# adaLN linear-attention block with a SiLU MLP on one core: first modulation columns as matrix products, later modulation sums by 32 by 32 transposes, and a new order table

## The chip, the core and the metric

The kernel runs on one core of one Trainium2 chip. The metric is the device time of one execution in microseconds (us). Every time below is from the runs of the kernel before the change, or from the profile of one of its executions.

## The reference

Inputs: `x` (2048 x 576), `wqkv` (576 x 1728), `wo` (576 x 576), `w1` (576 x 4608), `w2` (4608 x 576), `c` (1 x 576), `w_mod` (576 x 3456), all float32.

```python
mod = (silu(c) @ w_mod).reshape(1, 6, 1, 576)
sa, ca, ga, sb, cb, gb = (mod[:, i] for i in range(6))
h = layernorm(x) * (1 + ca) + sa
x = x + ga * linear_attention(h, wqkv, wo)     # 32 heads of 18, phi(t) = (t+1 if t>0 else exp(t)) + 1e-6
h = layernorm(x) * (1 + cb) + sb
x = x + gb * (silu(h @ w1) @ w2)
```

## The kernel before

**Tiling.** The 2048 rows are 16 tiles of 128, in four blocks of four. The width 576 is cut into five chunks k: four of 128 and a tail of 64, which is kept twice (128 wide) so that every chunk fills the partitions. Projections use pairs of values (a rounded part and the rest), so that each float32 product is made of several passes. In the trace one true float32 product (`x8` warm-ups in the program, say) appears as two matmul records, a transpose or a pass on rounded operands as one.

**Stages.** (1) The start: `c` goes through silu, the first two rows of the modulation (sa, ca; piece 0) are needed as columns (`cols["a"]`) because h is used transposed, tiles 0 and 1 are normalised, transposed on TensorE (`turn_tiles`), modulated (`modulate`, L355 to L361) and split (`split_h`), and their K projections run chunk by chunk (`first_k`, `k_lo`, `k_part` at L573). (2) The rest of the attention (to about 196 us): K projections of all tiles and Q projections of tiles 0 to 10 (L928), sums over tokens (L1053, added up on VectorE at L1063), the other pieces of the modulation (`mod_steps`, L1090: piece 1 is ga and sb, piece 2 is cb and gb), then `kv_steps` (L1178), whose mask is applied on VectorE at L1193, and `m_steps` (L1215), which multiplies the masked result with `wo`. (3) Attention outputs and second normalisation (to about 355 us). (4) The MLP, in 18 groups of 256 columns by two pairs of blocks (L1924, L2008), to the end.

**The start in detail.** `mods[k]` holds rows of `w_mod` for chunk k, `sc` is silu(c), `tmod` the tail rows, `sel` two columns that pick the two halves of the tail. `HEAD` = 2 chunks come first. The sum over k is made on VectorE: `add_rows` (L516, L518) multiplies `mods[k]` with its column of `sc` and adds into `sums`; then a product with a column of ones (`mod_cols`, L523 and L527) sums over partitions and yields columns of chunks 0 and 1. For chunks 2 to 4 the same sums give two rows on one partition (`mod_rows`, L538), these are copied to SBUF (`copy_row`), and turned into columns by six transposes of one row (`turn_rows`, L549). `add_cols` (L532) adds the 1 of (1 + ca). `keep_busy(n)` (L567) issues n products of ones, whose results nobody reads.

**Pieces 1 and 2.** `mod_steps` scales each chunk on ScalarE, adds chunks on GpSimd into `tmod` (128 partitions x 1152), stores it to DRAM (`parts`, L1104), loads it back so that each partition holds nine columns of all 128 partitions (L1107), reduces over them on VectorE (L1110), and stores `vec` (L1111).

**Order.** Inside stage 2 a table (`STAGE_A`) says in which order the steps of a small planner are issued. After the program is written, `arrange(ORDERS, begun)` takes, for each engine, the list of its instructions and ties them to the order of a second table of numbers, `ORDERS`, which reaches from the start into the first MLP units. Instructions on one engine wait in that order.

Of the kernel before, what the change touches and what calls it, by code (L numbers as in the profile page):

```python
# [24 lines left out]
def kernel(ctx: ExitStack, tc, A_x, A_wqkv, A_wo, B_x, B_w1, B_w2, c, w_mod, out):  # L25
# [33 lines left out]
    def behind(instructions):  # L59

        with ExitStack() as order:
# [7 lines left out]
            0-43 45-46 52 49-50 44 47-48 53-54 51 65 57-58 61-62 66-72 55-56 59-60 63-64 73-77 82-83 80-81 78-79  # L69
            84-87 90-91 88-89 92-101 116-118 102-103 124 104-105 119-123 125 106-115 126-141 154-167 142-153  # L70
            168-181 246-251 210-213 182-199 214-215 290-293 216-219 294-295 200-209 220-221 256-267 274-277
            222-223 278-289 224-237 302-307 238-245 252-255 308-311 268-273 330-335 296-301 336-357 312-319
            358-359 320-325 360-367 326-329 368-375 378-383 376-377 386-389 384-385 398-403 390-393 404-405
            394-397 412-423 436-451 406-411 424-435 452-477 490-499 478-489 524-527 500-513 520-523 530-539
            514-519 586-587 528-529 588-589 540-545 554-571 576-579 592-597 590-591 598-599 610-621 600-609
            546-551 646-647 580-581 622-627 582-585 552-553 572-575 648-657 670-671 628-641 672-675 682-683
            642-645 684-687 714-721 658-663 722-723 664-665 692-693 666-669 688-689 694-713 724-725 676-679
            726-727 690-691 728-729 680-681 742-745 730-741 746-791 826-831 792-795 862-863 796-797 864-867
            832-833 872-873 798-813 838-839 814-815 840-853 816-821 854-855 822-823 856-859 874-877 860-861
            868-871 878-889 834-837 890-895 824-825 896-917 926-935 918-921 936-939 922-923 940-947 924-925  # L80
            978-983 1000-1003 950-955 966-975 1004-1005 976-977 984-993 948-949 994-999 1006-1019 1022-1023
            1020-1021 956-965 1024-1035 1050-1055 1036-1049 1056-1063 1084-1085 1064-1077 1102-1105 1086-1087
            1106-1113 1078-1079 1114-1117 1088-1091 1118-1123 1130-1131 1080-1081 1132-1135 1124-1129 1136-1137
            1082-1083 1138-1155 1096-1099 1092-1095 1160-1169 1156-1157 1170-1171 1100-1101 1172-1183 1158-1159
            1184-1219 1236-1237 1248-1259 1220-1221 1285-1286 1222-1227 1238-1247 1228-1235 1287-1296 1260-1262
            1297-1300 1263-1284 1301-1325 1352-1356 1326-1349 1357-1364 1385-1388 1365-1370 1389-1390 1350-1351
            1371-1384 1413-1416 1391-1400 1417-1427 1401-1406 1428-1429 1407-1412 1430-1443 1446-1449 1444-1445
            1451-1468 1450 1479-1486 1469-1478 1507-1511 1487-1506 1512-1535 1540-1544 1536-1539 1545-1568
            1573-1574 1569-1572 1575-1592 1601-1604 1593-1594 1605-1621 1595-1596 1634 1638 1597-1600 1622-1633
            1646-1649 1635-1636 1650 1639-1641 1655-1660 1687-1696 1637 1661-1676 1642-1645 1677-1682 1715-1719  # L90
            1697-1700 1651-1654 1701-1704 1683 1705-1706 1720-1723 1684-1686 1707-1714 1724-1751 1762-1767
            1776-1779 1781-1782 1768-1769 1780 1752-1753 1783-1794 1754-1761 1795-1798 1770-1772 1799-1800
            1773-1775 1801-1810 1821-1825 1854 1870-1873 1855-1857 1826-1835 1811-1820 1836-1843 1874 1858
            1875-1877 1844-1853 1859-1860 1883 1915 1884-1886 1861-1863 1916-1918 1878-1881 1887-1888 1882
            1864-1869 1889-1914 1919-1921 1931-1935 1976 1922-1927 1936-1939 1928-1930 1990-1993 1940-1941 1994
            1977-1978 1995-1996 1942-1971 2004-2007 1972-1975 1979-1982 2008-2010 1983-1984 2011-2012 1985-1988
            2013-2018 1989 2019-2036 1997-2003 2037 2049-2061 2082-2083 2098-2101 2062-2069 2086-2088 2070-2077
            2038-2045 2084-2085 2046-2048 2078-2081 2089 2102-2103 2090-2093 2106-2110 2094 2111-2112 2104
            2113-2114 2095-2097 2115-2122 2105 2123-2140 2143 2141-2142 2147 2159-2166 2144-2145 2167-2172 2146
            2173-2178 2187 2179-2186 2188 2199-2202 2189-2190 2203 2191 2204-2210 2213-2214 2148-2149 2215-2216  # L100
            2192-2198 2211-2212 2150-2158 2217 2231-2234 2218-2223 2235-2238 2224-2230 2239-2241 2249 2259-2262
            2245 2255-2258 2246-2248 2242 2263-2264 2243-2244 2265-2269 2295 2250 2296-2299 2251-2253 2270
            2309-2313 2254 2283 2271 2284-2285 2277-2278 2286-2293 2300 2294 2301-2302 2314 2303 2279 2304-2308
            2272-2276 2280-2282 2315-2324 2329 2335-2338 2325 2339-2340 2330-2331 2326-2328 2341 2332-2334
# [498 lines left out]
    for k in (1, 2, 3):  # L603
        add_rows(k, 0, c1)
# [1806 lines left out]
```

## Time and profile before

| | us |
|---|---|
| median of 3 runs | 1084.69 |
| lowest, highest | 1081.81, 1085.14 |
| the profiled execution, its own time | 1086.77 |
| its span in the trace | 1085.1 |
| TensorE busy in the span | 1063.3 |
| VectorE busy | 893.0 |
| ScalarE busy | 707.3 |
| GpSimd busy | 737.6 |

The profile names engines PE (TensorE matmul), PEld (its weight loads), DVE (VectorE), ACT (ScalarE), POOL (GpSimd) and SP (the queue that issues most DMAs). A row of a timeline has the start, the time from the first to the last end, engine, line, operation, output<-inputs and count; in brackets stands how long the engine was idle before it and who ended that. The profiled execution is 1.6 us longer than its span, and 2.1 us longer than the median.

### The profile page before, as it was taken

The page shows a single profiled execution, that of the slowest core. Times are in us where ns is not written, and L with a number is a line of the kernel's source. Part 1 is how long each engine was busy: PE and PEld are TensorE (multiplying, and loading weights), DVE is VectorE, ACT ScalarE, POOL GpSimd, SP SyncE. Part 2 cuts the span into 40 slices and gives each one's busy share as a digit, 9 for nine tenths or more (in the row PEclk, how much of TensorE's full clock was granted, in tenths as well). Part 3 has the DMA queues.
Part 4 walks back from the last instruction along what each step waited for, and adds up shares of the span by engine and source line. Part 5 has one row for each costly group of instructions (what it writes and reads, how often), then busy time and mean ns, then how long its engine had stood idle before and what let it go on. Part 6 is the DMA issues. An engine that isn't in the chain of part 4 may idle for free.

```text
span 1085.1 us, 19052 instructions
## 1 busy us (share of the span) xinstructions
PE 1063.3 (98%) x7027; PEld 760.6 (70%) x7027; DVE 893.0 (82%) x1438; ACT 707.3 (65%) x1318; POOL 737.6 (68%) x804
## 2 busy tenths in 40 slices
PE   8999999999999899999999999999999999999998
PEld 6999999898885455666666666666666666666665
DVE  7966857788889899988987988987987887898767
ACT  4866553248667777777667667767766776676554
POOL 3467524654725589879888778877778678677563
PEclk9999999999999999999999999999999999999999
DMA  8497954224256877387577577567667657626422
GB/s 294 143 178 202 101 148 119 70 83 127 61 165 195 240 250 254 125 250 230 175 223 213 182 217 222 171 223 203 200 196 234 201 154 252 206 68 201 165 80 109
DMA packets 119341, 193.50 MB, mean 178 GB/s; under 512 B 42892, under 2 KB 77584, under 8 KB 119248
## 3 DMA queue, kind: packets, MB, share of 16 engines
q1 hardware_dynamic: 86276, 190.81, 56.6%
q10 hardware_dynamic: 32972, 1.48, 3.1%
q8 instruction: 55, 0.90, 0.4%
q14 instruction: 38, 0.31, 0.1%
HBM read 176.77 MB, written 15.48 MB: 177 GB/s over the span
## 4 chain that ended last, share of the span: by engine, by line
PE 80%; DVE 9%; DMA 4%; ACT 2%; POOL 2%; issue 1%; SPq 0%; DVEq 0%; POOLq 0%; ACTq 0%
PE up L1924 31%; PE down L2008 30%; PE big L389 5%; PE psK L928 4%; PE psG L1053 4%; PE big L1443 2%; DMA raw<-parts 1%; DMA hT<-hd 1%; PE small L1432 1%; DVE hT L261 1%; PE small L374 1%; DMA raw<-in_w_mod_dram 1%; DVE w L261 1%; PE big L1357 1%; PE psK L1223 1%
## 5 line engine op out<-in xcount | busy, mean ns | idle before, releaser
L1924 PE MATMUL up<-hT,w 128*128 128x512 f16 x1264 | 317.9, 379 | 2.2 <-DMA hT<-hd 2.2
L1924 PEld LDWEIGHTS <-w 128*128 128x128 f16 x1492 | 145.8, 98 | 136.1 <-DMA hT<-hd 2.9
L2017 DVE SCALAR_TENSOR_TENSOR acc<-acc,set,down 128x576 f32<-128x576 f32 x128 | 103.6, 810 | 33.8 <-PE down L2008 32.9
L1942 ACT ACTIVATE f<-f,set 128x512 f32<-128x512 f32 x102 | 73.3, 719 | 63.6 <-DVE f L1948 52.1
L1962 POOL TENSOR_TENSOR s<-f,f 128x256 f32<-128x256 f32 x66 | 54.6, 827 | 77.4 <-ACT f L1943 75.3
L2008 PE MATMUL down<-w,hc 128*128 128x288 f16 x600 | 90.6, 286 | 0.1
L2008 PE MATMUL down<-w,hb 128*128 128x288 f16 x600 | 89.3, 286 | 0.6 <-DVE U L2019 0.5
L2008 PE MATMUL down<-w,hT 128*128 128x288 f16 x480 | 82.8, 286 | 0.4 <-DVE acc L2021 0.4
L1946 DVE TENSOR_TENSOR f<-up,p 128x512 f32<-128x512 f32 x102 | 69.6, 682 | 13.8 <-PE up L1924 9.4
L1943 ACT ACTIVATE f<-f,set 128x512 f32<-128x512 f32 x102 | 73.6, 722 | 3.2
L2008 PEld LDWEIGHTS <-hb 128*128 128x128 f16 x600 | 58.7, 98 | 22.7 <-issue 1.4
L2008 PEld LDWEIGHTS <-hc 128*128 128x128 f16 x600 | 58.7, 98 | 22.0 <-issue 0.4
L1986 POOL TENSOR_TENSOR hc<-s,hc 128x512 f16<-128x512 f32 x50 | 63.9, 1278 | 6.0 <-ACT hc L1982 6.0
L1948 DVE TENSOR_TENSOR f<-up,f 128x512 f32<-128x512 f32 x68 | 46.8, 689 | 25.4 <-PE up L1924 24.3
L2008 PEld LDWEIGHTS <-hT 128*128 128x128 f16 x480 | 46.9, 98 | 26.6 <-issue 0.8
L1966 POOL TENSOR_TENSOR f<-f,s 128x256 f32<-128x256 f32 x66 | 53.4, 809 | 17.3 <-DVE hb L1986 10.2
L1959 POOL TENSOR_TENSOR s<-f 128x256 f32<-128x256 f32 x66 | 57.0, 864 | 9.5 <-ACT f L1939 4.5
L1964 POOL TENSOR_TENSOR s<-s,f 128x256 f32<-128x256 f32 x66 | 56.3, 853 | 3.5
L389 PE MATMUL big<-w,qT 128*128 128x288 f32 x352 | 58.6, 304 | 0.0
L2008 PE MATMUL down<-w,hd 128*128 128x288 f16 x396 | 55.5, 286 | 0.2 <-DVE acc L2017 0.2
L2008 PE MATMUL down<-w,ha 128*128 128x288 f16 x396 | 55.7, 286 | 0.0
L1053 PE MATMUL psG<-w,xs 128*128 128x288 f32 x336 | 52.2, 296 | 1.3 <-DVE sum L1063 1.3
(408 smaller groups left out, 2805.3 us busy)
## 6 DMA issues: line engine op xcount, KB each, us to landing
hT<-hd SPq DMA_DIRECT2D x101, 640.0 KB, 4.6
hT<-hd SPq DMA_DIRECT2D x65, 512.0 KB, 3.7
hT<-in_B_w_dram SPq DMA_DIRECT2D x14, 576.0 KB, 6.4
hT<-in_B_w_dram SPq DMA_DIRECT2D x28, 256.0 KB, 5.8
raw<-in_B_w_dram SPq DMA_DIRECT2D x11, 576.0 KB, 6.2
v<-in_B_w_dram SPq DMA_DIRECT2D x9, 576.0 KB, 4.9
acc<-in_A_x_dram SPq DMA_DIRECT2D x16, 288.0 KB, 4.3
raw<-in_B_w_dram SPq DMA_DIRECT2D x9, 512.0 KB, 5.2
```

Source lines behind the costliest of these rows:

```text
L389: T.matmul(ps, xpart(a), wpart(b), start=n == 0, stop=n == len(XW) - 1)
L1053: T.matmul(ps[:, h, :HALF], l, pk[t][:, u, h * HALF : (h + 1) * HALF], start=t == 0 and m == 0, stop=t == 3 and m == len(left) - 1)
L1924: T.matmul(ps, left, right, start=first and m == 0, stop=m == len(seq) - 1, skip_group_check=True)
L1942: A.activation(f, f, AF.Silu, scale=factor(self.g, "inv"))
L1943: A.activation(f, f, AF.Identity, scale=factor(self.g, "delta"))
L1946: V.tensor_add(f, self.bank[bank[1]], self.p1)
L1959: G.tensor_sub(self.s3, half(i, 0, 0), half(i, 0, 1))
L1962: G.tensor_add(self.s[:, 0:1], half(i, 0, 1), half(i, 1, 1))
L1964: G.tensor_sub(self.s[:, 1:2], self.s[:, 0:1], half(i, 0, 0))
L1986: eng.tensor_sub(t[:, :, 1, :], src, t[:, :, 0, :])
L2008: T.matmul(ps[:, p, :HALF], left[:, u, p * P : (p + 1) * P], right[:, v], start=n in (1, 5, 7, 6) and j == 0, stop=j == len(passes) - 1, s ...
L2017: V.scalar_tensor_tensor(dst, dst, factor(self.g, "ratio"), ps[:, :, :HALF], op0=ALU.mult, op1=ALU.add)
```

## The change

Piece 0 is no longer summed on VectorE. Each of the five chunks of the two rows becomes a group of products whose stationary operand is a 128 x 128 block of `mods[k]` and whose moving operand is the column of `sc`, repeated 64 times (chunks 0 and 1) or 42 times (chunks 2 to 4); all land in one PSUM bank, and `add_cols` takes one of the equal columns. `twice` copies the 64 tail columns on GpSimd so that the last chunk is 128 wide. Rows, copies and one-row transposes go. For pieces 1 and 2, `tmod` is transposed in blocks of 32 by 32 on VectorE, reduced over groups of 32, transposed again, and only a 128 x 64 tile goes through DRAM (`quarters`) to add the four quarters. One weight load is issued ahead of two loads of `x`. `ORDERS` is a new table for all engines; `STAGE_A` stays.

```diff
     load_w(0, range(HEAD, KC))
+    load_w(0, [KC])
     xts += [load_x(i) for i in range(2, 4)]
-    load_w(0, [KC])
...
+    WIDE = 64, 42
+    def twice(m):
+        G.tensor_copy(m[..., D:DX], m[..., KC * P : D])
+    def mod_tail(js):
+        for j in js:
+            for a in range(2):
+                o = col(j, a)
+                T.matmul(o, tmod[:, j * P : (j + 1) * P], sel[:, a : a + 1].to_broadcast([P, o.shape[1]]),
+                         start=j == js[0] and a == 0, stop=False, skip_group_check=True)
+    def mod_part(k, js):
+        for j in js:
+            for a in range(2):
+                o = col(j, a)
+                T.matmul(o, mods[k][:, a, j * P : (j + 1) * P], sc[:, k : k + 1].to_broadcast([P, o.shape[1]]),
+                         start=False, stop=k == KC - 1, skip_group_check=True)
...
     keep_busy(11)
-    for k in range(HEAD):
-        mod_cols(k, tmod, sel, first=k == 0)
+    mod_tail(range(HEAD))
+    for k in range(KC):
+        mod_part(k, range(HEAD))
     turn_tiles(pT, (0, 1), START)
-    for k in (1, 2, 3):
-        add_rows(k, 0, c1)
+    keep_busy(4)
+    add_cols(0, HEAD)
...
+    twice(tmod)
+    mod_tail(range(HEAD, KC + 1))
+    for k in range(KC):
+        twice(mods[k])
+        mod_part(k, range(HEAD, KC + 1))
+        keep_busy(1)
+        if k < HEAD:
+            first_k(k)
     keep_busy(2)
+    add_cols(HEAD, KC + 1)
...
-        do("SP", 0.45, lambda: nc.sync.dma_start(parts, tmod2[:, :, 0:D]), ["tmod0", "tmod1"], [f"parts{piece}"], 8.0)
-        do("DVE", 2.27, lambda: V.tensor_reduce(s9, r.rearrange("q p j -> q j p"), axis=AX.X, op=ALU.add), raws2[i], [f"s9{piece}"])
+        def turn():
+            for a in range(2):
+                V.transpose(r[:, a].rearrange("p (b i) -> p b i", i=32), tmod2[:, a, 0:D].rearrange("p (b i) -> p b i", i=32))
+        def fold():
+            V.tensor_reduce(some[:, 0:NB32], flat.rearrange("p (b i) -> p b i", i=32), axis=AX.X, op=ALU.add)
+            V.transpose(turned_sums, some)
+            nc.sync.dma_start(quarters.rearrange("h p c -> p h c"), turned_sums.rearrange("p (h c) -> p h c", h=2))
+            for h in range(2):
+                n = (32, NB32 - 32)[h]
+                nc.sync.dma_start(four[32 * h : 32 * h + n], quarters[h].rearrange("(q b) c -> b q c", q=4)[:n])
+            V.tensor_reduce(total, four.rearrange("b q c -> b c q"), axis=AX.X, op=ALU.add)
```

**How the order moves: the start on TensorE.** The rows stand on TensorE behind the eleven warm-ups and the transposes of tiles 0 and 1, before the change (`psG_116`, `psG_117` and `psK` are PSUM, `xt` holds normalised rows of x, `hT` is the room of `mods` in products with `ones` or `sc`, and of h in products with `w`):

```order
L567 MATMUL psG_117<-ones 128x128 x4
L527 MATMUL psG_116<-ones,hT 128x1 x2
L567 MATMUL psG_117<-ones 128x128
L527 MATMUL psG_116<-ones,hT 128x1 x2
L567 MATMUL psG_117<-ones 128x128 x2
L573 MATMUL psK<-w,hT 128x288 x3
L538 MATMUL psG_116<-tmod,sc 1x320
L573 MATMUL psK<-w,hT 128x288 x7
L538 MATMUL psG_117<-tmod,sc 1x320
L538 MATMUL psG_117<-hT,ones 1x320
L573 MATMUL psK<-w,hT 128x288 x4
```

The end of the same stretch now, from the last groups of narrow products on (20 products 64 wide, ten transposes but one, and 18 products 42 wide stand ahead of these rows):

```order
L531 MATMUL psG_117<-sc,hT 128x42 x6
L542 MATMUL psG_116<-ident,xt 128x128
L553 MATMUL psG_117<-ones 128x128
L531 MATMUL psG_117<-sc,hT 128x42 x6
L553 MATMUL psG_117<-ones 128x128 x4
L1239 MATMUL psG_117<-ident,xt 128x128 x2
L559 MATMUL psK<-w,hT 128x288 x7
L1239 MATMUL psG_116<-ident,xt 128x128 x8
L559 MATMUL psK<-w,hT 128x288 x29
```

Before, the first projections (L573) stood between the steps that make the columns of chunks 2 to 4; now all 50 narrow products (20 of 64 columns, 30 of 42) stand ahead of the first projection (L559), and no projection waits for a column inside that stretch.

**The end of stage 2 on TensorE.** The rows are the last products of `kv_steps` and the first of `m_steps`, before:

```order
L1186 MATMUL psG_116<-sum_107,acc_94 72x72
L1186 MATMUL psG_116<-sum_108,acc_94 72x72
L1186 MATMUL psG_116<-sum_109,acc_94 72x72
L1186 MATMUL psG_116<-sum_110,acc_94 72x72
L1186 MATMUL psG_116<-sum_111,xt 72x72
L1223 MATMUL psK<-raw_121,tmod 128x288 x5
L1223 MATMUL psK<-raw_122,tmod 128x288
```

And now:

```order
L1175 MATMUL psG_116<-sum_109,acc_94 72x72
L1175 MATMUL psG_116<-sum_110,acc_94 72x72
L1175 MATMUL psG_116<-sum_111,xt 72x72
L901 MATMUL psK<-wq,hT 128x288 x12
L901 MATMUL psK<-v,hT 128x288 x4
L1212 MATMUL psK<-raw_121,tmod 128x288 x5
L1212 MATMUL psK<-raw_122,tmod 128x288
```

Sixteen passes of a Q projection, which stood ahead of `kv_steps` or among its products, now stand between its last product and the first of `m_steps`.

More of the change, by code (lines that the diff above doesn't have):

```diff
@@ L74 @@
[L74 to L78, printed above, removed]
@@ L186 @@
+            207
         """,
@@ L500 @@
     wk_ = wkp
-    sums = mods[0]
     sel = z[:, 2:4]
@@ L615 @@
     w_lo(wk_, 0, acc[0], G)
[L616 to L633 removed]
+    for k in range(HEAD):
+        modulate(*args[k], V)
+        split_h(*args[k])
+    w_hi(wk_, 1, acc[1])
+    w_lo(wk_, 1, acc[1], V)
+    twice(tmod)
[6 more added lines that the diff above has]
+            first_k(k)
+    keep_busy(2)
+    add_cols(HEAD, KC + 1)
     k_lo(0)
@@ L835, in follow @@
                         self.ops[queue.pop(0)][2]()
+                assert len(made) > before
         def emit(self):
@@ L1090, in mod_steps @@
     def mod_steps(piece):
-        parts, vec = parts_of[piece - 1], vec_of[piece - 1]
+        quarters, vec = quarters_of[piece - 1], vec_of[piece - 1]
         for k in START:
```

311 lines of the change are left out of this document (134 added, 177 removed).

## The prediction

> **What bounds the kernel now.** I read the page first, for the engine that fills the span.
>
> ```profile
> span 1085.1 us, 19052 instructions
> ...
> PE 1063.3 (98%) x7027; PEld 760.6 (70%) x7027; DVE 893.0 (82%) x1438; ACT 707.3 (65%) x1318; POOL 737.6 (68%) x804
> ```
>
> TensorE (PE) is busy for 1063.3 of 1085.1 us, so a gain can only come from the 21.8 us in which it is idle, from PE work that goes, or from a higher granted clock. The second view, busy time by stage, says where the idle time is (the columns are the stretch and its length, then PE, PEld, DVE, ACT and POOL busy, granted clock, DMA share, GB/s).
>
> ```profile
> 0.00:8.85 8.85, 7.46 (x39) 7.08 (x40) 3.35 (x17) 3.77 (x7) 1.44 (x8) 1.00 0.76 217
> 8.85:33.77 24.92, 21.27 (x132) 16.30 (x131) 22.08 (x46) 14.01 (x27) 10.05 (x7) 0.93 0.84 284
> 33.77:60.00 26.23, 25.50 (x188) 24.88 (x187) 21.84 (x35) 20.96 (x33) 15.87 (x11) 1.00 0.55 169
> ...
> 195.90:210.00 14.10, 12.17 (x62) 10.00 (x62) 11.01 (x28) 4.49 (x7) 6.66 (x7) 1.00 0.24 66
> ...
> 250.00:400.00 150.00, 142.59 (x947) 104.24 (x947) 133.81 (x231) 105.87 (x190) 82.45 (x90) 1.00 0.56 174
> 400.00:1000.00 600.00, 599.51 (x3801) 371.55 (x3799) 516.03 (x793) 422.97 (x841) 479.85 (x564) 1.00 0.64 201
> 1000.00:1085.10 85.10, 80.43 (x548) 53.31 (x546) 59.81 (x87) 44.73 (x75) 45.30 (x45) 1.00 0.35 120
> ```
>
> From 400 to 1000 us PE has 0.5 us left and nothing that an order table does there can matter. The idle time is 3.65 us in the start (24.92 less 21.27), 0.7 up to 60, 1.9 around 200, and 7.4 from 250 to 400, where VectorE (DVE) is busy for 133.81 of 150 us and is the engine waited for. The waits of PE by releaser agree:
>
> ```profile
> PE up L1924 <- DMA hT<-hd: 2.2, 1, 2.2
> PE big L1443 <- DVE acc L1448: 1.9, 1, 1.9
> PE psG L1053 <- DVE sum L1063: 1.3, 2, 0.7
> PE psK L1223 <- issue: 1.2, 1, 1.2
> ```
>
> The start also loses clock. A finer table shows PE 0.70 of 2 us busy from 18 to 20, and the clock at half from there to 24:
>
> ```profile
> 18.00:20.00 2.00, 0.70 (x2) 0.09 (x2) 2.00 (x2) 0.48 (x3) 1.85 (x2) 1.00 1.02 319
> 20.00:22.00 2.00, 1.81 (x6) 0.65 (x6) 1.93 (x7) 1.18 (x3) 0.00 (x0) 0.71 1.06 335
> 22.00:24.00 2.00, 2.00 (x9) 1.78 (x8) 1.24 (x4) 0.00 (x0) 1.69 (x2) 0.50 1.04 328
> ```
>
> **The start, step by step.** The stretch to price runs from the end of the eleven warm-ups (8.85) to the first pass of a Q projection at L928 (33.77). The same two points exist after the change, with all work between them in one line on PE. Its rows today:
>
> ```profile
> 8.85 0.58 PE L523 MATMUL psG<-z,tmod 128*128 128x2 f32 x4
> ...
> 10.69 0.44 PE L556 MATMUL psK<-ident,xt 128*128 128x128 f32 x2 [0.66 <-ACT xt L351]
> 10.97 0.49 PE L556 MATMUL psG<-ident,xt 128*128 128x128 f32 x3
> 11.29 1.06 PE L567 MATMUL psG<-ones 128*128 128x128 f32 x8
> 12.19 0.50 PE L527 MATMUL psG<-ones,hT 128*128 128x1 f32 x4
> 12.55 0.47 PE L567 MATMUL psG<-ones 128*128 128x128 f32 x2
> ```
>
> ```profile
> 28.19 2.38 PE L573 MATMUL psK<-w,hT 128*128 128x288 f32 x16 [0.20 <-DVE hT L261]
> 30.41 0.43 PE L573 MATMUL psK<-v,hT 128*128 128x288 f32 x2
> ...
> 31.79 0.82 PE L1250 MATMUL psG<-ident,xt 128*128 128x128 f32 x6
> 32.37 0.77 PE L573 MATMUL psK<-w,hT 128*128 128x288 f32 x4
> ...
> 33.77 0.47 PE L928 MATMUL psK<-wq,hT 128*128 128x288 f32 x2
> ```
>
> Durations overlap, so I price by the distance of starts. A float32 product is two records. With one moving column it takes (12.55 - 12.19)/2 = 0.18 us, with 128 columns (12.19 - 11.29)/4 = 0.225 us. The new products have 64 and 42 columns and lie between these: 0.18 to 0.225, and I take 0.20. A transpose takes (11.29 - 10.69)/5 = 0.12 us, one of the later ten (32.37 - 31.79)/6 = 0.10. A pass of a projection takes (30.41 - 28.19)/16 = 0.139 us.
>
> [...]
>
> After the change: 50 narrow products at 0.20 are 10.0 us; 10 transposes at 0.12 are 1.2; the warm-ups between them (4, three single ones, 4: eleven) at 0.225 are 2.5; ten later transposes at 0.10 are 1.0; the 56 passes of the two K projections at 0.139 are 7.8. The sum is 22.5 us, and with 0.4 for small waits 22.9, against 24.92 now: **2.0 us gained**. It is no more because only 3.65 us are idle and about 1.7 are lost to 3.4 us at half clock, while PE gets roughly 4 us of new work. By the two prices of a narrow product (9.0 or 11.25 us) the gain is 0.8 to 3.0.
>
> What has to hide for this: the loads of `mods` and weights. DMA moves 284 GB/s in this stretch, and the two parts of `mods` now come before the weights, so the last weight comes later, and it is waited for late. DVE makes column adds and `modulate` under the first four, then under the last four warm-ups; if that cover (1 us) is too thin, the first wait is for L559 passes of chunk 2, which stand behind 16 passes and 8 transposes, 3 us later. The five GpSimd copies of 64 columns are under the first products.
>
> **VectorE behind the start.** What leaves DVE is grouped here:
>
> ```profile
> L518 DVE SCALAR_TENSOR_TENSOR hT<-hT,sc 128x512 f32<-128x512 f32 (+1 forms) x6 | 5.9, 986 | 0.1
> ...
> L516 DVE TENSOR_SCALAR hT<-hT,sc 128x512 f32<-128x512 f32 (+1 forms) x2 | 1.4, 712 | 1.7 <-DMA hT<-in_w_mod_dram 1.7
> ```
>
> That is 7.3 us out of 22.08 that DVE is busy in the stretch. From 33.77 to 60 PE waits 0.73 us for results that DVE and ACT bring late. With DVE 7 us ahead I take **0.5 us** of it; bounds 0 and 0.7.
>
> **Pieces 1 and 2.** On DVE the reduction of 2.39 us goes. Two transposes of 576 columns, a contiguous reduction of 1152, and two small operations come, twice.
>
> ```profile
> 83.14 2.76 DVE L1020 STREAM_TRANSPOSE acc<-xt 128x576 f32<-128x576 f32 x4
> 87.44 2.39 DVE L1110 TENSOR_REDUCE crow<-raw 128x9 f32<-128x1152 f32 x1 [1.53 <-DMA raw<-parts]
> ```
>
> ```profile
> L757 DVE TENSOR_REDUCE crow<-bc_gb x2: 740/742/743, 165.3 to 189.8; 128x1 f32<-128x576 f32 x2
> ```
>
> The DMAs of today, by the views of two tiles (from issue to landing), first the large load and then the small stores of a column:
>
> ```profile
> L1107 ACTq DMA_DIRECT2D raw<-parts x2: 400/408/416, 71.2 to 119.5; - x2
> ...
> DMA to landing us min/median/max: 13.9/13.9/13.9
> ```
>
> ```profile
> L1111 SPq DMA_DIRECT2D vec<-crow x2: 332/414/497, 94.9 to 141.1; - x2
> ...
> DMA to landing us min/median/max: 4.1/5.4/7.0
> ```
>
> A transpose is 0.69 us, a reduction of 576 columns 0.74, so a piece costs 1.4 + 1.5 + about 0.4 = 3.3 us, 0.9 more than now. It lies between 60 and 130 us, where DVE has idle time; PE waits for it only through its queue. What the chain of waits held there was a DMA: `raw<-parts` landed 13.9 us after its issue, behind a store. Now two small DMAs stand in its place; those of `vec` landed after 4.1 to 7.0 us. That pulls the second piece forward by about 10 us, and of the 1.3 us that PE waits for L1063 I take one of two waits, **0.6 us**; bounds -0.6 and 1.3.
>
> **The end of stage 2.** Here the last product of `kv_steps` is followed by three DVE operations and then by `m_steps`:
>
> ```profile
> 195.62 0.29 PE L1186 MATMUL psG<-sum,xt 128*72 128x72 f32 x2
> ...
> 196.23 0.68 DVE L1193 TENSOR_TENSOR tmod<-psG,h 126x504 f32<-126x504 f32 x1
> ...
> 197.11 6.54 PE L1223 MATMUL psK<-raw,tmod 126*128 126x288 f32 x26 [1.20 <-issue]
> ```
>
> The table now puts sixteen passes of a Q projection (16 x 0.139 = 2.2 us) in the gap of 1.2 us, and they are passes that had to run anyhow: **1.2 us**. Their former places, among the sums, are filled by other sums. Bounds 0.5 (if those places now wait) and 1.2.
>
> **The rest of the table** moves rows on every engine up to about 400 us. I count it as nothing, with 7.4 us of idle time there as the bound on the gain, and as much on the loss.
>
> **The sum.** 2.0 + 0.5 + 0.6 + 1.2 = 4.3 us. The profiled execution's own 1086.77 us would become 1082.5; it stood 2.1 us above the median of 1084.69, so as a median I say **1080.4**.
>
> **Rivals.**
>
> *The clock falls in the narrow products (slower).* The clock fell after a window with little streaming through the array, not only after idle time: from 18 to 20 us PE was busy a third of the time. A product of 42 columns streams a third of one of 128, and these fill 14 to 23 us with few warm-ups between. The 13.7 us of products, transposes and warm-ups would take up to twice as long: 13.7 lost, 1094. Each 3.4 us at half clock costs 1.7, so the change turns into a loss after 8.6 us of it. Against it: products of one column ran from 12.19 on with warm-ups among them, and the clock held until 20. [...]
>
> *VectorE's order from 250 to 400 is worse (slower).* DVE has 16 us free in 150. Each of its operations (0.7 to 0.8 us) that is put ahead of one that PE waits for costs its length; the 7.4 us idle could double and a little more: 8 lost, 1088.4. It decides from 4.3 us on, five or six such places. For it: much of this stretch is reordered. Against it: the sequence of sums and adds that PE waits for there (L1684, L1685, L1448) stands nearly as before.
>
> *The table also takes out half of the idle time from 250 to 400:* 3.7 more, 1076.7.
>
> *The narrow products cost as much as wide ones, or wait for loads:* the start gives nothing; 1082.4.
>
> *The head start is given back:* PE comes 4 us early to a DMA or a DVE result that keeps its own time, as the 2.2 us for `hT<-hd` shows; 1084.
>
> **How the numbers follow.** The forecast has 0.50, with a range of its own of 1077.5 to 1083; clock 0.07, DVE order 0.13, more idle time gone 0.10, dear products 0.08, given back 0.12. About 0.3% (3.25 us) is what a measurement of this kernel can tell from no change: faster is below 1081.4, slower above 1087.9. Of the forecast 0.37 is below 1081.4, so faster is 0.37 + 0.10 + 0.01 for the best of the dear products = 0.48; slower 0.07 + 0.13 = 0.20; the rest 0.32. The range is 1076 to 1088.5: it reaches to the DVE rival and leaves out the clock rival and tails of the others.
>
> **What would show it.** In the changed profile the first L901 pass starts near 31.8 us; the narrow products' starts are 0.09 to 0.11 us per record apart; no stretch below 1.00 of clock between 9 and 32 us. The first L1212 row follows L901 with no idle time. The transposes at L1086 take 0.69 us, and the DMAs of `quarters` land in 4 to 7 us. Idle time of PE from 250 to 400 stays near 7 us. A clock of 0.50 in the start, a start of L901 past 33.8, or over 11 us of idle time from 250 to 400 would make the prediction wrong.

## The result and the profile after

The changed kernel takes 1095.74 us (median of 4 executions, 1093.20 to 1100.76) against 1084.91 us before (4 executions, 1081.81 to 1085.83): ratio 1.0111, 95% interval 1.0066 to 1.0155. Forecast was 1080.4 us; it became **slower by 1.1%**, outside the range of 1076 to 1088.5.

The profiled execution took 1093.91 us with a span of 1092.2 us, 7.1 us longer than the span of before. From the page of the changed kernel:

```profile
span 1092.2 us, 19208 instructions
...
PE 1070.1 (98%) x7095; PEld 768.9 (70%) x7095; DVE 886.3 (81%) x1435; ACT 706.5 (65%) x1316; POOL 736.5 (67%) x809
```

TensorE (PE) is busy 6.8 us longer than before (1063.3) and idle as long as before (22.1 us against 21.8). Where the time went is seen at points that both programs have:

| start of | before | changed | difference |
|---|---|---|---|
| first Q pass (L928, now L901) | 33.77 | 33.47 | -0.3 |
| first pass of an MLP unit (L1924, now L1913) | 356.99 | 361.56 | +4.6 |
| last `down` passes (L2008, now L1997) | 1068.06 | 1075.39 | +7.3 |

So in this execution the start gained almost nothing, 4.9 us are lost between Q and the first unit, and 2.7 us in the units. The busy time by stage of the changed kernel (columns as in the prediction) has the same stretches, and one more around 333 us:

```profile
8.85:33.77 24.92, 24.02 (x200) 23.16 (x199) 15.29 (x42) 16.37 (x31) 10.94 (x13) 1.00 0.80 270
33.77:60.00 26.23, 23.25 (x161) 22.78 (x160) 20.33 (x25) 17.66 (x28) 14.29 (x10) 0.93 0.48 140
195.90:210.00 14.10, 14.10 (x85) 11.88 (x85) 8.40 (x21) 3.85 (x7) 5.60 (x6) 1.00 0.10 30
250.00:400.00 150.00, 143.79 (x943) 104.36 (x942) 134.57 (x231) 105.53 (x188) 83.63 (x84) 0.99 0.54 177
400.00:1000.00 600.00, 595.72 (x3773) 368.80 (x3773) 513.69 (x789) 416.93 (x827) 474.20 (x563) 1.00 0.64 199
...
331.20:334.60 3.40, 3.40 (x13) 1.70 (x12) 2.84 (x5) 1.74 (x3) 2.46 (x3) 0.55 0.75 307
```

The start is full (24.02 of 24.92 us) at clock 1.00, and yet no shorter: it is PE work now. Behind it PE is idle for 3.0 us up to 60, the clock falls there and at 331 us, and from 400 to 1000 us PE is idle for 4.3 us where it was 0.5. The waits of PE name the places:

```profile
PE up L1913 <- DMA hT<-hd: 3.5, 3, 2.1
PE psK L901 <- DVE v L479: 2.9, 1, 2.9
...
PE small L376 <- DVE xn L355: 1.1, 1, 1.1
```

The new rows of the start on PE, and the wait behind it:

```profile
8.54 1.10 PE L524 MATMUL psG<-z,tmod 128*128 128x64 f32 x8
9.48 1.28 PE L531 MATMUL psG<-sc,hT 128*128 128x64 f32 x10
10.60 0.28 PE L542 MATMUL psK<-ident,xt 128*128 128x128 f32 x1
...
17.87 0.47 PE L553 MATMUL psG<-ones 128*128 128x128 f32 x2
18.17 1.43 PE L531 MATMUL psG<-sc,hT 128*128 128x42 f32 x12
19.43 0.47 PE L553 MATMUL psG<-ones 128*128 128x128 f32 x2
19.73 1.43 PE L531 MATMUL psG<-sc,hT 128*128 128x42 f32 x12
...
22.62 0.91 PE L553 MATMUL psG<-ones 128*128 128x128 f32 x6
23.79 0.49 PE L553 MATMUL psG<-ones 128*128 128x128 f32 x2 [0.26 <-DVE col_a L537]
24.11 0.38 PE L1239 MATMUL psG<-ident,xt 128*128 128x128 f32 x2
...
33.47 4.27 PE L901 MATMUL psK<-wq,hT 128*128 128x288 f32 x30 [0.33 <-ACT e L908]
...
43.38 0.80 PE L901 MATMUL psK<-v,hT 128*128 128x288 f32 x4 [2.90 <-DVE v L479]
```

A product of 64 columns takes (10.60 - 9.48)/5 = 0.224 us, one of 42 columns (19.43 - 18.17)/6 = 0.21.

The other three executions took 1093.20, 1097.56 and 1100.76 us; their mean granted clocks were 0.997, 0.994 and 0.989 against 0.997 in the profiled one. 3.4 us at half clock are 1.7 of some 1092 us, or 0.0016 of the mean: by this estimate there were two such stretches in the profiled execution and in the one of 1093.20 us, four and seven in the other two. The profile shows the mildest case.

### The profile page after: what moved, and what is told of

It reads as the page before. It is cut to its first block, busy times and chain, and to the rows that moved or that the text cites. A ratio compares the mean times of both kernels' runs of the same rounds, so it can differ in the third digit from the quotient of the medians.

```text
span 1092.2 us, 19208 instructions
## 1 busy us (share of the span) xinstructions
PE 1070.1 (98%) x7095; PEld 768.9 (70%) x7095; DVE 886.3 (81%) x1435; ACT 706.5 (65%) x1316; POOL 736.5 (67%) x809
## 4 chain that ended last, share of the span: by engine, by line
PE 61%; DVE 4%; ACT 2%; DMA 1%; issue 1%; POOL 0%; DVEq 0%; POOLq 0%
PE up L1913 30%; PE down L1997 29%; DMA hT<-hd 1%; DVE w L269 1%; PE down L2031 1%; PE up L2031 1%; DVE acc L1437 1%; DVE acc L2010 0%; DVE hb L1975 0%; ACT f L1931 0%; ACT f L1932 0%; DVE f L1937 0%; DVE f L1935 0%; DVE hs L269 0%; ACT w L1601 0%
## 5 line engine op out<-in xcount | busy, mean ns | idle before, releaser
L1913 PE MATMUL up<-hT,w 128*128 128x512 f16 x1264 | 318.4, 379 | 3.9 <-DMA hT<-hd 3.5
L1913 PEld LDWEIGHTS <-w 128*128 128x128 f16 x1492 | 145.7, 98 | 137.7 <-DMA hT<-hd 4.4
L1997 PE MATMUL down<-w,hb 128*128 128x288 f16 x600 | 90.3, 286 | 0.1
L1997 PE MATMUL down<-w,hc 128*128 128x288 f16 x600 | 89.9, 286 | 0.1
L1997 PE MATMUL down<-w,hT 128*128 128x288 f16 x480 | 82.8, 286 | 0.4 <-DVE acc L2010 0.4
L1997 PEld LDWEIGHTS <-hb 128*128 128x128 f16 x600 | 58.7, 98 | 22.7 <-issue 0.3
L1997 PEld LDWEIGHTS <-hc 128*128 128x128 f16 x600 | 58.7, 98 | 22.5 <-issue 0.4
L1997 PEld LDWEIGHTS <-hT 128*128 128x128 f16 x480 | 47.0, 98 | 26.6 <-issue 0.8
L391 PE MATMUL big<-w,qT 128*128 128x288 f32 x352 | 57.4, 304 | 0.0
L1997 PE MATMUL down<-w,ha 128*128 128x288 f16 x396 | 56.2, 286 | 0.0
L1997 PE MATMUL down<-w,hd 128*128 128x288 f16 x396 | 55.8, 286 | 0.4 <-POOL hd L1975 0.4
```

The source lines that it names most:

```text
L391: T.matmul(ps, xpart(a), wpart(b), start=n == 0, stop=n == len(XW) - 1)
L1913: T.matmul(ps, left, right, start=first and m == 0, stop=m == len(seq) - 1, skip_group_check=True)
L1997: T.matmul(ps[:, p, :HALF], left[:, u, p * P : (p + 1) * P], right[:, v], start=n in (1, 5, 7, 6) and j == 0, stop=j == len(passes) - 1, s ...
```

## The experiments

All medians stand beside executions of the kernel before on the same chip (1084.5 to 1084.8 us). "Columns" is the first part of the change, "sums" the second. Where an order is edited only the numbers that move are shown.

| run | median us | ratio to before, 95% | first Q pass, span in the profile |
|---|---|---|---|
| changed_again | 1097.46 | 1.0113 (1.0084 to 1.0142) | 40.77, 1097.8 |
| v_first | 1095.88 | 1.0095 (1.0067 to 1.0122) | 37.60, 1090.8 |
| gpsimd_moved | 1097.01 | 1.0105 (1.0085 to 1.0126) | 39.31, 1095.9 |
| new_order_to_213 | 1091.89 | 1.0064 (1.0040 to 1.0088) | 33.68, 1088.4 |
| new_code_old_tail | 1091.08 | 1.0061 (1.0040 to 1.0082) | 33.60, 1087.3 |
| columns_only | 1088.85 | 1.0040 (1.0025 to 1.0056) | 39.60, 1087.1 |
| more_warmups | 1087.32 | 1.0040 (1.0018 to 1.0062) | 44.18, 1092.2 |
| one_column | 1096.24 | 1.0097 (1.0080 to 1.0114) | 42.38, 1091.1 |
| passes_between | 1088.41 | 1.0037 (1.0019 to 1.0056) | 43.01, 1091.3 |
| sums_only | 1089.27 | 1.0045 (1.0029 to 1.0062) | 34.18, 1087.6 |
| sums_later | 1085.82 | 1.0006 (0.9991 to 1.0020) | 32.41, 1082.4 |
| columns_and_sums | 1092.23 | 1.0053 (1.0034 to 1.0072) | 38.77, 1085.8 |

### v_first: VectorE's order at 36 to 43 us

One number of VectorE's (DVE) row of the changed order moves:

```diff
-  44 31 45 39 46 72 48 54 41 53 55 50 47 52 75
+  44 31 45 39 46 72 48 54 41 47 53 55 50 52 75
```

> The changed kernel with one place of VectorE's order changed: the second L479 (the remainder of v, 64 rows) stands directly behind the L477 at 36.84 us instead of behind two L263 and L952. Theory A (the loss sits on VectorE between 36 and 43 us, where its two-input operations are stretched while GpSimd is busy, and PE waits 2.9 us for v and then runs 3.4 us at half clock): the wait of L901 for L479 falls from 2.9 us to under 0.6, the half clock of 43 to 47 us goes, the span falls by 4 to 4.6 us to about 1088, 0.3% above the kernel before. Rival B (what PE gains there is taken back later, since another engine or a transfer keeps its own time): the wait goes, but the first L1212 row stands less than 1 us earlier than 200.42 and the span stays at 1091 to 1092. Rival C (v is late by its own inputs): the wait stays above 2 us.

The wait for v went, as A said, but the median is 1095.88 us against 1095.74: B holds. From the first Q pass to the first L1212 row it is 204.12 - 37.60 = 166.5 us against 200.42 - 33.47 = 166.9; a wait of 1.93 us for L908 at 49.57 us, and half clock behind it (a mean clock of 0.57 from 50 to 52 us), took the place of the other. What no theory had named: the first Q pass came at 37.60 us, since the clock of the start fell to half, 19.6 to 29.8 us. One execution had a mean clock of 1.000, so no half clock at all: it took 1088.90 us, still 4.4 us above the kernel before. The clock is not all of the loss.

### gpsimd_moved: why VectorE was late

```diff
-  10 20 16 18 15 17 19 23 21 22 26
+  10 20 16 18 19 23 21 15 17 22 26
```

> The changed kernel with two GpSimd instructions (the L938 pair, 38.2 to 40.9 us) moved behind the two L1076 additions that follow the second L935. Theory H (two-input operations of VectorE wait out a GpSimd operation that runs at that time): relative to the first Q pass, GpSimd is free from about +6.2 us on, the two L263 take 0.4 to 0.7 us each after the second L935 has ended instead of 2.45 together, L952 takes 0.2 to 0.25 us instead of 1.41, and PE's wait for v is 1.0 to 1.6 us instead of 2.9. Rival (the operations are long for a reason of their own): L952 stays above 1 us and the wait above 2.5 us.

VectorE in the changed kernel, and below it GpSimd (POOL) at the same time:

```profile
36.84 1.99 DVE L477 TENSOR_TENSOR wq<-acc,wq 128x576 fp32r<-128x576 f32 x1
38.75 2.45 DVE L263 TENSOR_TENSOR hT<-raw,hT 128x256 fp32r<-128x256 f32 x2
41.13 1.41 DVE L952 TENSOR_TENSOR xs<-xt,xs 128x64 fp32r<-128x64 f32 x1
42.57 0.76 DVE L479 TENSOR_TENSOR v<-acc,v 64x576 fp32r<-64x576 f32 x1
```

```profile
36.62 1.59 POOL L935 TENSOR_TENSOR w<-a,w 128x576 fp32r<-128x576 f32 x1 [2.07 <-DVE a L496]
38.16 1.20 POOL L938 COPY zsum<-a 128x576 f32<-128x576 f32 x1
39.43 1.49 POOL L938 TENSOR_TENSOR zsum<-zsum,a 128x576 f32<-128x576 f32 x1
40.88 1.58 POOL L935 TENSOR_TENSOR w<-a,w 128x576 fp32r<-128x576 f32 x1
```

And VectorE with the pair moved, when GpSimd stands still from 46.94 to 54.22 us:

```profile
45.24 1.98 DVE L263 TENSOR_TENSOR hT<-raw,hT 128x256 fp32r<-128x256 f32 x2
47.14 0.21 DVE L952 TENSOR_TENSOR xs<-xt,xs 128x64 fp32r<-128x64 f32 x1
47.38 0.76 DVE L479 TENSOR_TENSOR v<-acc,v 64x576 fp32r<-64x576 f32 x1
```

L952 fell from 1.41 to 0.21 us and PE's wait for v from 2.90 to 1.23, as H said. The two L263 fell only from 2.45 to 1.98 us together; the second L935 of GpSimd still stood beside the first of them, from 45.41 to 46.94. In the changed kernel L952 began at 41.13 and ended at 42.54, just behind GpSimd's L935 (42.46). The time as a whole did not fall (1097.01 us): from the first Q pass to the first L1212 row it is 167.1 us.

### new_code_old_tail, new_order_to_213, changed_again: code or order

The first has the changed code, the changed order up to 34 us and the old order behind it; the second the changed order up to 213 us; the third is the changed kernel, unedited. The first two edit only the table:

```diff
     ORDERS = {
-        (the changed order)
+        (the changed order up to 34 or 213 us, from there the rows of the kernel before)
```

> The changed kernel's code and its order up to 34 us; from there on every engine's instructions stand in the order of the kernel before (the new transposes, reductions and small DMAs of the sums stand where the store, the load and the reduction of the old ones stood). Theory A (the reordering behind the start costs the 7 us, the code costs nothing): the first Q pass starts at 33.4 to 33.6 us, no wait above 1 us before 60 us, span 1084 to 1086, no difference from before. Rival D (the new code is the cost, the order repairs part of it): span 1090 us or more, with the waits at the places of the sums, 60 to 200 us.

> The changed kernel with its own order up to 213 us and the order of the kernel before behind it. From the first L391 pass to the end the changed order took 882.3, 877.2 and 880.0 us in three profiles, the old order 875.2 to 877.7 in six. Theory K (the reordering behind 213 us costs 2 to 5 us: the waits for hT<-hd and L355): from the first L391 pass to the end 875 to 877 us; the median falls below the changed kernel's by 3 to 5 us, 1090 to 1093. Rival (those differences come with the execution, not with the order): 879 us or more, median 1095 or more.

> The changed kernel once more, unedited, for the spread of its executions. If the clock of the start decides (it held from 9 to 33 us in the profiled execution and fell in the same instructions in two others), the times lie in two groups, about 1091 to 1094 without the fall and 1096 to 1101 with it, and this profile has a first Q pass either near 33.5 us or past 37 us. If not, they lie within 0.3% of each other.

With its own order up to 213 us the kernel takes 1091.89 us, and 1097.46 as changed, on the same chip: the order behind 213 us costs **5.6 us** by the medians. Each has six executions, which spread over 7 and 12 us; ordered by time, the changed ones lie 3.7 to 7.9 us above their counterparts. K holds for the stretch, and the median fell by a little more than its 3 to 5 us. From the first L391 pass (L389 in new_order_to_213) to the end it is 1088.4 - 212.96 = 875.4 us against 1092.2 - 209.87 = 882.3 in the changed kernel and 1097.8 - 217.22 = 880.6 in its second profile. The other two profiles with the changed order there have 880.0 (gpsimd_moved) and 877.2 (v_first); ten with the old order have 875.2 to 877.7. So the price differs from one execution to the next, and v_first lies within the old order's range. The first pass in new_order_to_213 and in the second profile of the changed kernel:

```profile
212.96 1.06 PE L389 MATMUL big<-wq,hT 128*128 128x288 f32 x6
```

```profile
217.22 1.06 PE L391 MATMUL big<-wq,hT 128*128 128x288 f32 x6
```

The line for `hT<-hd` (an activation that comes back from HBM for an `up` pass) has 3.2 us in two waits in the second profile of the changed kernel, and 0.4 us with the old order:

```profile
PE up L1913 <- DMA hT<-hd: 3.2, 2, 1.7
```

```profile
L1911 PE MATMUL up<-hT,w 128*128 128x512 f16 x1264 | 318.0, 379 | 0.4 <-DMA hT<-hd 0.4
```

Between 34 and 213 us old and new order cost the same (ratios to before of 1.0061 and 1.0064, each on its own chip), though the waits differ; so neither theory of new_code_old_tail was right. That run was slower by 0.6%, by the place of the sums (below) and by the start's clock in other executions: 1087.5 to 1089.3 in four, 1092.9 to 1095.0 in four.

changed_again came in two groups, 1091.27 to 1095.42 and 1099.49 to 1102.89 us, three each. Its profile is one of the second group, and the same instructions as before are stretched from 20.16 us on; the columns are the stretch, then busy times, and the clock stands third from the end:

```profile
8.85:20.16 11.31, 11.06 (x97) 10.87 (x96) 4.12 (x14) 5.59 (x10) 4.38 (x8) 1.00 1.04 386
20.16:33.80 13.64, 13.38 (x64) 13.07 (x62) 5.43 (x16) 4.73 (x10) 2.74 (x2) 0.50 0.37 103
33.80:40.77 6.97, 6.77 (x52) 6.54 (x50) 5.34 (x13) 5.80 (x12) 3.85 (x4) 1.00 0.45 137
```

### columns_only, more_warmups, one_column, passes_between: the clock

columns_only is the kernel before with the columns, and the old order behind 34 us. The others edit it:

```diff
     mod_tail(range(HEAD, KC + 1))
+    keep_busy(2)                    (more_warmups)
     for k in range(KC):
         twice(mods[k])
         mod_part(k, range(HEAD, KC + 1))
-        keep_busy(1)
+        keep_busy(3)                (more_warmups)
...
-    WIDE = 64, 42
+    WIDE = 1, 1                     (one_column)
```

and passes_between moves sixteen L559 passes in PE's order.

> The kernel before with the first part of the change alone: modulation columns by narrow products, with the changed kernel's order up to 34 us and the order of the kernel before behind it; the old sums with the 13.9 us load stay. By my sum of the start as it came out (first Q pass 0.3 us earlier than before): span 1084.5 to 1085.5. If VectorE's head start of 7 us is worth something as I forecast, 0.5 less. Rival: the narrow start leaves weights or hT later than the old order behind it wants them; then a wait of 1 us or more between 33 and 60 us and a span of 1087 or more.

> The first part alone, as in the run with the columns alone, with ten warm-ups more between the narrow products of 42 columns (two behind the first six products, three instead of one behind each of the four groups of twelve records). They cost 10 x 0.225 = 2.25 us at full clock. Theory E (the clock falls where the window of the throttle sees mostly 42-column products, and the run of the columns alone lost 6 us of its start to that): the clock stays at 1.00 from 9 to 35 us, the first Q pass starts at 35.6 to 36.2 us instead of 39.60, each execution's mean clock is 0.996 or more, and the median is 1 to 2 us lower, 1087 to 1088. Rival F (the clock falls for another reason, such as the eviction and the idle 0.26 us at 15 us, or the load of the whole chip): half clock from 19 us on as before, first Q pass near 42 us, median 1089.5 or more.

> The first part alone with products of one column in place of 64 and 42 (the same instructions in the same order; the column read is the same). Theory E: less streams through the array, so that the clock falls earlier, within the first group too (before 17 us) and stays down to the K passes; first Q pass past 41 us, median 1089 to 1091; before the fall a product takes 0.18 to 0.20 us against 0.21 to 0.22. Rival F (width has no part in it): the fall comes at 19 us as with 42 columns, the first Q pass stays within 0.5 us of 39.6.

> The first part alone, with sixteen passes of the K projection (L559, chunks 0 and 1, 288 columns) moved from behind the narrow products to between them: eight behind the third group of 42-column products, eight behind the fourth. No work is added. In the runs so far the half clock that began at 19 to 21 us lasted until the K passes ran, 9 to 16 us later, and ten more warm-ups did not shorten it. Theory J (it is these passes that bring the clock back): half clock of 3.4 to 7 us at most, over by 28 us, first Q pass at 33.5 to 36.5 us instead of 39.60, median 1085 to 1087. Rival (the clock comes back after a time of its own): half until past 30 us, first Q pass past 38 us, median 1088.5 or more.

columns_only is 0.4% slower, and its first Q pass comes 5.8 us late, not 0.3 early. The span of 1087.1 us is in the rival's range, but not for its reason: from 33 to 60 us PE waits 0.2 us. It is the clock:

```profile
8.85:19.20 10.35, 9.97 (x90) 9.81 (x90) 4.30 (x14) 5.59 (x11) 4.32 (x8) 1.00 1.04 387
19.20:32.84 13.64, 13.38 (x63) 13.07 (x63) 5.50 (x16) 4.65 (x10) 2.89 (x2) 0.50 0.43 133
32.84:39.60 6.76, 6.53 (x50) 6.30 (x49) 5.18 (x14) 5.79 (x12) 3.57 (x4) 1.00 0.47 137
```

PE is busy all through the half clock (13.38 of 13.64 us), and ahead of it for 9.97 of 10.35 us, so idle time is not what keeps it down. With ten more warm-ups eight executions took 1086.05 to 1088.06 us and four 1093.88 to 1095.01. E is right for the eight, wrong for the four, of which the profile is one:

```profile
19.48:36.56 17.08, 16.82 (x79) 16.51 (x79) 4.10 (x11) 4.90 (x11) 1.51 (x1) 0.50 0.32 97
```

With one column the clock falls earlier, at 13.7 us, and stays down 20.5 us, as E said. All six executions have mean clocks of 0.987 to 0.991, and the median of 1096.24 us lies above the 1089 to 1091 that E gave. The price of a product did not fall:

```profile
9.44 1.26 PE L531 MATMUL psG<-sc,hT 128*128 128x1 f32 x10
10.55 0.31 PE L542 MATMUL psK<-ident,xt 128*128 128x128 f32 x1
```

1.11/5 = 0.22 us for a product of one column, at full clock: its price is not that of its width. The clock did differ with the width: the instructions are the same as in columns_only (run on another chip), and by the mean clocks about twice as much time is lost (0.009 to 0.013 of full clock against 0.005 to 0.007).

With K passes between the products five executions took 1084.4 to 1085.9 us, as fast as before, four 1087.7 to 1090.8 and three 1092.7 to 1093.0. Six of the twelve have a mean clock of 1.000, none of the five of columns_only (0.993 to 0.995, on another chip). In the profile of passes_between the half clock lasted past two groups of eight passes, which J excluded:

```profile
17.88:38.36 20.48, 19.76 (x89) 19.06 (x89) 6.69 (x20) 7.44 (x16) 2.97 (x3) 0.50 0.38 121
```

What ends it is not settled: in columns_and_sums the first eight passes, from 23.20 us on, stood in the last 3.41 us before it ended at 26.00.

The record shows what differs between executions of one start. Within a profile the changes of the clock lie whole steps of 3.41 us apart: the falls of the changed kernel's at 44.10 and 330.82 us by 84 steps, those of gpsimd_moved's at 10.80 and 21.04 by three. The steps lie elsewhere against the program in each execution: one comes 2.34 us behind the start of the first single warm-up (L553) in the changed kernel's profile, 0.84 in changed_again's. Counted back by seven steps from the fall at 44.10 us, one step of the changed kernel's runs from 16.79 to 20.21 us: it holds the single warm-ups at 17.87 and 19.43 us, and the clock held. In columns_only, with the same start on PE, the step from 15.77 to 19.18 us holds only one, at 18.28, and the clock fell at its end:

```profile
18.28 0.47 PE L553 MATMUL psG<-ones 128*128 128x128 f32 x2
```

In new_order_to_213, whose start held the clock too, the same step (17.57 to 20.99 us, seven ahead of the fall at 44.88) has two such warm-ups, at 18.07 and 19.64; in changed_again (19.32, fall at 20.16) and gpsimd_moved (19.50, fall at 21.04) it has one. It is no fixed count, since the profile of more_warmups lost the clock at 19.48 us behind a step with two whole ones (four records from 17.67 on) and the start of a third. What decides was not shown.

### sums_only, sums_later: the transposes

sums_only is the kernel before with the sums; sums_later moves the second piece on VectorE and SP:

```diff
 (VectorE's order, second piece)
-  ... hT L1001 x3, acc L496, [transpose x2, reduce, transpose], hT L1001, ...     at 112 us
+  ... w L964 x2, [transpose x2, reduce, transpose], sum L1067, ...                at 134 us
```

> The kernel before with the second part alone: the sums of pieces 1 and 2 by 32 by 32 transposes, placed where the store of the parts stood (transposes) and where the old reduction stood (last reduction); all else in the old order. My forecast of this part was 0.6 us gained with bounds -0.6 and 1.3: the waits of L1053 for L1063 (1.3 us) fall to 0.7 or less, span 1084 to 1086. Rival: VectorE, which takes its operations in order, stands still at the last reduction until the two small DMAs have landed; then an idle time of VectorE of 3 us or more before that reduction, and a span of 1087 or more.

> The second part alone, with the transposes and the reduction of the second piece moved from 112 us (ahead of the hT that PE waited 1.8 us for) to the 4.4 us in which VectorE stood idle in the kernel before (133.7 to 138.1), its last reduction to 147.5, and its small DMAs to match; the first piece stays. Theory G (what the sums cost is 3.0 us of VectorE in one piece ahead of a result that PE needs, and the half clock that follows the wait): the wait for hT and the half clock at 113 to 117 us go, L1053's waits for sums stay near 1.3 us, and the span is 1084 to 1085.5, as before. Rival: the chain vec, columns, rows of the second piece is now 7 us later and PE or the first MLP unit waits for it: span 1087 or more.

VectorE in sums_only, and PE:

```profile
112.87 1.42 DVE L1117 STREAM_TRANSPOSE raw<-tmod 128x576 f32<-128x576 f32 x2
114.32 1.35 DVE L1120 TENSOR_REDUCE crow<-raw 128x36 f32<-128x1152 f32 x1
115.71 0.24 DVE L1121 STREAM_TRANSPOSE raw<-crow 128x64 f32<-128x64 f32 x1
115.88 0.65 DVE L1001 TENSOR_TENSOR hT<-h,hT 128x512 fp32r<-128x512 f32 x1
```

```profile
116.58 0.74 PE L932 MATMUL psK<-v,hT 128*128 128x288 f32 x2 [1.82 <-DVE hT L1001]
```

3.0 us of VectorE stand ahead of an hT that PE needs; PE waits 1.82 us and then runs at half clock (a pair of passes starts every 0.49 us from 117.12 us on, and every 0.26 ahead of the wait). The last reduction, which the rival named, did not wait (in the changed kernel the small DMAs land in 1.7 to 3.2 us). Moved by 22 us, the same work costs nothing that can be measured (1085.82 us, 0.9991 to 1.0020): G holds. This run also shows what half clock cost the old start:

```profile
15.80:22.60 6.80, 6.80 (x18) 2.93 (x17) 5.21 (x10) 2.34 (x5) 4.23 (x4) 0.51 1.06 333
...
32.41 3.80 PE L932 MATMUL psK<-wq,hT 128*128 128x288 f32 x27
```

6.8 us at half clock, twice as much as in the kernel before, and the first Q pass at 32.41 us, 1.4 us earlier than there. The waits of 0.90 and 0.71 us for VectorE that the kernel before has at 18.78 and 20.19 us are absent here: in the old start, stretched passes stood where PE would wait.

### columns_and_sums: all parts at better places

Both parts with the passes between, the later sums and the old order elsewhere.

> Both parts of the change, with the sixteen K passes between the narrow products, the second piece's transposes in VectorE's idle time at 134 us, and the old order everywhere else behind 34 us. If clock, VectorE's queue and order were all of the loss, it is as fast as the kernel before or faster: span 1081 to 1084.5, median 1083 to 1086. If the new code has a cost that none of these runs has shown: median 1088 or more.

The two executions at 1086.95 and 1087.49 us (the latter is the profile, with only 6.8 us at half clock in the start) and the four at 1092.00 to 1092.99 leave the median of 1092.23 us where the expectation put a cost that no other run has shown (1088 or more). The four have mean clocks of 0.993 or 0.994, so the clock is part of it. The one of 1086.95 us has 1.000 and is still 2.3 us above before; what that is stays open. In the profile the first Q pass is 5.0 us late. No version that was run beats the kernel before.

## Why the prediction was wrong, step by step

Two steps carry most of the error. The rest of the table was put at nothing and costs 5.6 us behind 213 us. The start was booked as 2.0 us of gain at full clock, with a chance of 0.07 that the clock falls; it gained nothing where the clock held, and the columns with their clock cost 4.3 us (columns_only). Both stand below with the other terms.

**The start (-2.0).** In the profiled execution, where the clock held, the stretch that the sum prices gained nothing: from 8.54 to 33.47 us it is 24.9 us, as long as the 24.92 of before and not the 22.9 of the sum. (The first Q pass is 0.3 us earlier because the stretch began 0.3 earlier.) Three terms were too small. The 50 products took 10.7 us, not 10.0. The eleven warm-ups with their waits took 3.7 us, not 2.9 with all waits: twice PE waits 0.26 us for VectorE's `col_a`, and a warm-up between products costs 0.30 (19.43 to 19.73). The 56 projection passes with the wait ahead of the first Q pass took 8.4 us, not 7.8. My lower price of a product, 0.18 us, came from one of two groups of products of one column; the other, of the same form, gives (13.41 - 12.95)/2 = 0.23:

```profile
12.95 0.61 PE L527 MATMUL psG<-ones,hT 128*128 128x1 f32 x4
13.41 0.69 PE L567 MATMUL psG<-ones 128*128 128x128 f32 x4
```

And one_column shows 0.22. The rival with dear products was thus right about the start: the 0.21 to 0.224 measured lie near the upper of the prediction's two prices (0.225), and I had taken 0.20.

**The clock rival (0.07, 1094).** This chance was far too low. In the three profiles in which the start held (the changed kernel's first, new_code_old_tail, new_order_to_213) the first Q pass comes at 33.5 to 33.7 us; in the eight others with narrow products it comes at 37.6 to 44.2 us, after 6.8 to 20.5 us at half clock. I had counted against it that the old products of one column ran at clock 1.00 until 20 us; but there the clock did fall then (20.8 to 24.2 us), and sums_later suggests why that cost little: PE was waiting for VectorE anyway. I had booked those 3.4 us as a gain of the change. The new start moves VectorE's work onto PE, and 3.4 us at half clock there can cost up to 1.7 us by the prediction's estimate. The rival's price was too high, since some of the loss is given back: columns_only starts Q 5.8 us late and ends 2.0 us late. Of these 3.8, 1.8 are the wait for `hT<-hd` at 374 us, 2.17 before and 0.34 there. That its 1094 lies near the measured 1095.74 is luck: the profiled execution took 1093.91 us with the start at clock 1.00 throughout.

**VectorE's head start (-0.5).** It became a wait of 2.9 us for v and 3.41 us at half clock behind it (44.10 to 47.51 us). The working of the forecast asked how many microseconds VectorE has to do, not which engine runs beside it: its two-input L952 took 1.41 us beside GpSimd's L935 (the rows at 41.13 and 40.88 us) and 0.21 us in gpsimd_moved, where GpSimd stood still; the two L263 took 2.45 us together and 1.98. Removing the wait alone gave nothing (v_first), so it isn't the cause of the total.

**Pieces 1 and 2 (-0.6).** In the changed kernel the size is right, by luck in part: one of two waits for a sum was to go, both went (1.3 us before), and two for w of 0.8 us together came, so -0.5. The price of a piece, read in sums_only, is as worked out (1.42 + 1.35 + 0.24 + 0.34 = 3.35 us against 3.3), and the small DMAs were faster than the 4.1 to 7.0 us taken for them (1.7 to 3.2). The bound of -0.6 on the other side was too narrow: sums_only is 4.7 us slower, by the place of the second piece (sums_later).

**The end of stage 2 (-1.2).** L1212 follows without idle time, as forecast, but 1.06 us of waiting now stand among the products of `kv_steps` (L1175):

```profile
194.00 0.45 PE L1175 MATMUL psG<-sum,xt 128*126 128x126 f32 x2 [1.06 <-issue]
...
200.42 6.47 PE L1212 MATMUL psK<-raw,tmod 126*128 126x288 f32 x26
```

The wait for v at L389 (0.73) went too: -0.9 in all.

**The rest of the table (0).** This is the largest single cost. It was put at nothing, and behind 213 us it costs 5.6 us (the medians of changed_again and new_order_to_213); between 34 and 213 us no cost is seen. My bound of 7.4 us held, but I looked for the loss on VectorE from 250 to 400 us, and idle time fell there (7.4 to 6.2 us). What came is 3.4 us at half clock at 331 us, 1.7 us lost, behind two waits for `xn` (in one of the four profiles with this order), and, past 400 us where I had written that the table can do nothing, the waits for `hT<-hd`: 2.0 to 4.8 us of idle time there in the four profiles against 0.5 or 0.6. Which of SP's reordered transfers makes them late was not tried.

**The sum as measured:** changed_again's median lies 12.8 us above before's on its chip. Columns with their clock cost 4.3 us (columns_only) and the order behind 213 us 5.6, which leaves 2.9 for the sums at their place and the rest. These parts come from different chips and need not add up: the sums alone cost 4.7 us at one place and nothing that can be measured at another.

## What to carry to other kernels

An engine that fills 98% of the span still has stretches in which it waits, and half clock can hide there (sums_later: 6.8 us of it, and the first Q pass 1.4 us earlier than before); work moved onto it takes that cover away (columns_only: 13.64 us of it, and the first Q pass 5.8 us late), so price the clock again before booking its return as a gain. A sum over one profile doesn't tell how often the clock falls: look at the spread of the executions and their mean clocks, and profile a second one. For a reordering, ask which engine works beside the instruction that is waited for (L952: 1.41 us beside GpSimd's L935, 0.21 without) and what stands ahead of it on its own engine (3.0 us of VectorE in sums_only), and follow the transfers that the reordered rows issue beyond the end of the table.

## What the runs showed of the hardware

- The half clock came in multiples of 3.41 us: 3.4 (before), 6.8 (columns_and_sums), 10.2 (v_first), 13.64 (columns_only, changed_again), 17.08 (more_warmups), 20.48 (passes_between). A busy PE did not end it: in more_warmups PE was busy for 16.82 of the 17.08 us, mostly with float32 products and warm-ups. Products of the K projection (288 columns) ran shortly before it came back (from 33.12 us on in one_column, where it came back at 34.17, and from 34.68 on in more_warmups, where it came back at 36.56); but in passes_between sixteen of them, from 24.67 and 29.15 us on, did not bring it back before 38.36.
- Six executions of the changed kernel on one chip had mean clocks of 0.989 to 0.998, some seven stretches of 3.4 us at half clock to one by the estimate above; the profiled one of them spent 13.64 us of its start at half clock.
- A float32 product with 1 (one_column), 42 or 64 moving columns (the changed kernel) started every 0.21 to 0.224 us at full clock; in the kernel before two groups with one column gave 0.18 and 0.23.
- From the first MLP pass to the last `down` passes the old order takes 708.8 us in columns_only, 709.6 in sums_later and 711.1 in the kernel before; most of the difference is one wait for `hT<-hd`, of 0.34, 0.91 and 2.17 us. These passes begin at 361.50, 356.01 and 356.99 us, so how early PE comes does not set the wait alone.
